# Reordering the last outputs, the softmax and the W products of a fused attention and feed-forward kernel

## The chip, the cores and the metric

The kernel runs on one core of one Trainium2 chip. In it TensorE multiplies matrices and writes the products into PSUM, an on-chip memory; VectorE and ScalarE copy them out of it (an "eviction"); SyncE, ScalarE and GpSimd issue the transfers (DMA) to and from the chip's main memory. The metric is device time in microseconds (us) from start to end; lower is better. Each version is run several times and the median is quoted. One further execution is taken with the hardware profiler; its span is some 1.8 us shorter than the device time of the same execution (569.5 against 571.25 us for the kernel before).

## The reference, cut to what matters

```python
B, N, C = 4, 5824, 256                    # four batches; d_ff is 1024
qn = q / (norm(q, axis=1) + 1e-6);  kn = k / (norm(k, axis=1) + 1e-6)
a  = softmax(kn.transpose(0, 2, 1) @ qn / tau)     # 256 x 256 per batch
x  = (v @ a).reshape(B * N, C)
out = ((x @ w1) * (x @ w2)) @ w3 @ w_out           # 23296 x 256, float32
```

The kernel folds the softmax into w1 and w2 ("fold", giving Wf for each batch), and w3 @ w_out into one matrix W (the "W products"). What is left per row is a = v Wf1, b = v Wf2, and o = (a*b) W. In profile lines, s and e are the scaled scores and their exponential, w is a W product and w3T the transposed w3 that it needs; osb and oleft are the copies of o and of the left rows (below) that are stored.

## The kernel before

TensorE's instructions are written out in one order by a bookkeeping clock. A list of due times (`at`) says at which clock value a piece of softmax, of the scores or of W is put between the a/b steps. Each batch is cut into twelve chunks: eleven of 512 rows, and a small last one of 192 rows, of which 64 are "left rows" that two neighbouring batches share in one output tile.

```python
LAG = 2          # outputs o run this many steps behind a and b
LAG_END = 5      # ... in the last chunk of the last batch

# soft_units(n): (cost, due time after the scores, piece)
return (
    [(0.0, 0.0, norms), (0.0, 6.0, k_row)]
    + [(0.0, 6.0 + 1.3 * i, lambda i=i: k_step(i)) for i in range(4)]
    + [(0.0, 6.5, q_sums), (0.0, 9.3, lambda: q_norm(st["ss"]))]
    + [(0.0, 11.3 + 1.3 * ct, lambda ct=ct: scale(ct)) for ct in range(CT)]
    + [(0.0, 12.0 + 1.3 * ct, lambda ct=ct: exps(ct)) for ct in range(CT)]
    + [(0.2, 16.5, sums)]
    + [(0.43, 17.5 + 1.1 * i, lambda i=i: fold(i)) for i in range(8)]
)
# ... cut ...
def emit_ab(b, c, j):             # 4 matmuls; ScalarE casts a, VectorE multiplies it by b
    # ... cut ...
    nc.scalar.copy(a_sb[:, :n], tiles[0][:, :n])
    nc.vector.tensor_mul(ab, a_sb, tiles[1])
# ... cut ... emit_out, last step of a small chunk:
    nc.scalar.copy(o[:, 0, :], tl[0][:, 0, :])
    other = nc.scalar if b == B - 1 else nc.sync
    other.dma_start(out=rows[:, NT - 1, :], in_=o[:, 0, :])
    if b % 2 == 1:
        nc.vector.tensor_copy(o2, tl[1][:, 0, :])           # the left rows of two batches
        for k, eng in enumerate((nc.sync, other)):
            m = b - 1 + k
            eng.dma_start(out=out[m * N + NT * P : (m + 1) * N, :], in_=o2[k * LEFT : (k + 1) * LEFT, :])
# ... cut ... the main loop
    lag = LAG_END if b == B - 1 and c == NCH - 1 else LAG
    while w_ready[0] and len(pend) > lag and npop < 2:
        emit_out(*pend.pop(0))
# ... and after it
while pend:
    emit_out(*pend.pop(0))
```

Of the kernel before, what the change touches and what calls it, by code (L numbers as in the profile page):

```python
# [15 lines left out]
P = 128  # L16
PIECE = 8
LAG = 2
LAG_END = 5
# [6 lines left out]
def kernel(  # L26
# [12 lines left out]
    nc = tc.nc  # L39
# [204 lines left out]
    def soft_units(n):  # L244
# [37 lines left out]
        def k_step(i):  # L282
            kr = st["kr"]
            nc.scalar.activation(  # L284
                out=kr, in_=kr if i else st["row"], func=(AF.Ln, AF.Exp)[i % 2],
                scale=(1.0, 0.5, 1.0, -1.0)[i], bias=eps_t if i == 2 else 0.0,
            )
# [17 lines left out]
        def q_norm(src):  # L305
            r = work.tile([P, CT], F32, tag="r", name=f"r_{n}", bufs=2)
            nc.scalar.activation(out=r, in_=src, func=AF.Ln)
            nc.scalar.activation(out=r, in_=r, func=AF.Exp, scale=0.5)
            nc.vector.tensor_scalar_add(r, r, 1e-6)
            nc.vector.reciprocal(r, r)  # L310
            if inv_tau != 1.0:
                nc.vector.tensor_scalar_mul(r, r, inv_tau)
            st["r"] = r

        def scale(ct):
            if ct == 0:
                st["s"] = work.tile([P, CT, C], F32, tag="s", name=f"s_{n}", bufs=1)
            nc.vector.tensor_mul(st["s"][:, ct, :], G_tiles[n][:, ct, :], st["kr"])  # L318

        def exps(ct):  # L320
            if ct == 0:
                st["e"] = work.tile([P, CT, C], BF16, tag="e", name=f"e_{n}", bufs=2)
            nc.scalar.activation(  # L323
                out=st["e"][:, ct, :], in_=st["s"][:, ct, :], func=AF.Exp, scale=st["r"][:, ct : ct + 1]
            )
# [49 lines left out]
        def fold(i, tag="ab"):  # L375
            h, rest = divmod(i, 4)
            w, c1 = divmod(rest, 2)
            for c2 in range(CT):
                fold_mm((w, c1, h * 512, (h + 1) * 512), c2, tag, i % 2 == 0 or (n == 0 and i == 7))
# [36 lines left out]
        if n == 0:  # L416
            return [k_first, k_row, q_first, scaled_first, first_folds, second_quarter, sum_start] + [lambda i=i: fold(i) for i in range(4, 8)]

        return (
            [(0.0, 0.0, norms), (0.0, 6.0, k_row)]  # L420
            + [(0.0, 6.0 + 1.3 * i, lambda i=i: k_step(i)) for i in range(4)]
            + [(0.0, 6.5, q_sums), (0.0, 9.3, lambda: q_norm(st["ss"]))]
            + [(0.0, 11.3 + 1.3 * ct, lambda ct=ct: scale(ct)) for ct in range(CT)]
            + [(0.0, 12.0 + 1.3 * ct, lambda ct=ct: exps(ct)) for ct in range(CT)]
            + [(0.2, 16.5, sums)]
            + [(0.43, 17.5 + 1.1 * i, lambda i=i: fold(i)) for i in range(8)]
        )


# [12 lines left out]
    def at(t, cost, fn):  # L442
        seq[0] += 1
        agenda.append((t, seq[0], cost, fn))
# [55 lines left out]
        last_ab[0] = ab  # L500
        clock[0] += 4 * (n * MM_COL + MM_FIX)

    def emit_out(b, c, j, ab):
        small = c == NCH - 1
        if small:
            lhs = [ab[:, :P]]
            if b % 2 == 1:
                lhs.append(lefts[b // 2][:, j, :, :].rearrange("p b t -> p (b t)")[:, P : P + 2 * LEFT])
        else:
            lhs = [ab[:, i * P : (i + 1) * P] for i in range(4)]  # L510
        if j == 0:
            out_tiles[b, c] = [
                psum.tile([P, 2, D], F32, tag="out", name=f"o_{b}_{c}_{h}", bufs=3)
                for h in range(len(lhs) if small else 2)
            ]
        tl = out_tiles[b, c]
        for s, lhsT in reversed(list(enumerate(lhs))) if small else enumerate(lhs):
            h, o = (s, 0) if small else divmod(s, 2)
            nc.tensor.matmul(  # L519
                tl[h][:, o, :], lhsT=lhsT, rhs=W_sb[:, j, :],  # L520
                start=(j == 0 and o == 0), stop=(j == FT - 1 and (small or o == 1)),
                skip_group_check=True,
            )
        clock[0] += len(lhs) * (D * MM_COL + MM_FIX)
        if j == FT - 1:
            o = work.tile([P, 4, D], F32, tag="o_sb", name=f"osb_{b}_{c}", bufs=3)
            rows = out[b * N : b * N + NT * P, :].rearrange("(p i) c -> p i c", i=NT)
            if small:
                nc.scalar.copy(o[:, 0, :], tl[0][:, 0, :])
                other = nc.scalar if b == B - 1 else nc.sync  # L530
                other.dma_start(out=rows[:, NT - 1, :], in_=o[:, 0, :])
                if b % 2 == 1:
                    o2 = work.tile([P, D], F32, tag="kr", name=f"oleft_{b}", bufs=1)
                    nc.vector.tensor_copy(o2, tl[1][:, 0, :])
                    for k, eng in enumerate((nc.sync, other)):
                        m = b - 1 + k
                        eng.dma_start(out=out[m * N + NT * P : (m + 1) * N, :], in_=o2[k * LEFT : (k + 1) * LEFT, :])
            else:
                nc.scalar.copy(o[:, 0:2, :], tl[0])  # L539
                nc.vector.tensor_copy(o[:, 2:4, :], tl[1])  # L540
                nc.sync.dma_start(out=rows[:, 4 * c : 4 * c + 4, :], in_=o)
            del out_tiles[b, c]

    NDEF = 4

# [114 lines left out]
    def make_agenda(b):  # L660
        agenda.clear()
        clock[0] = 0.0
        n = b + 1
        if b == 0:
            at(0.5, 0.87, soft0[5])
            for i in range(4):
                at((1.7, 2.6, 3.5, 3.9)[i], 0.43, soft0[7 + i])
            at(0.0, 0.0, load_library)
            at(4.6, 0.5, lambda: transpose_half_on_pe(0, 0, 1, False))
            at(7.0, 0.5, lambda: transpose_half_on_pe(0, 1, 0, True))  # L670
            at(8.0, 0.5, lambda: transpose_half_on_pe(0, 1, 1, False))
            at(15.0, 0.0, transpose_w3)
            at(15.0, 0.0, lambda: transpose_piece(0, 2))
            for jt in range(FT):
                at(26.0 + 1.2 * jt, 0.87, lambda jt=jt: w_unit(jt))
            moves = [("qk", 1, 0, 29.0), ("v", 0, 3, 30.0), ("v", 0, 4, 30.5), ("qk", 1, 1, 44.0), ("qk", 1, 2, 45.0)]
            moves += [("qk", 1, 3, 53.0), ("qk", 1, 4, 55.0), ("v", 0, 5, 61.0), ("qk", 1, 5, 73.0)]
            moves += [("v", 1, 0, 88.0), ("v", 1, 1, 98.0), ("v", 1, 2, 120.0), ("qk", 2, 0, 130.0)]
            t0, t1 = 54.0, 113.0
        else:  # L680
            moves = [("v", b, 3, 1.0), ("qk", n, 1, 10.0), ("qk", n, 2, 17.0), ("v", b, 4, 26.0), ("qk", n, 3, 38.0)]
            moves += [("v", b, 5, 46.0), ("qk", n, 4, 58.0), ("qk", n, 5, 66.0)]
            moves += [("v", n, 0, 76.0), ("v", n, 1, 86.0), ("v", n, 2, 96.0), ("qk", n + 1, 0, 108.0)]
            moves = [m for m in moves if m[1] < B]
            t0, t1 = 16.0, 98.0

        before = (0, 2) if b == 0 else None
        for nm, m, pi, t in moves:
            if before is not None and not (nm == "v" and before == (m, pi - 1) == (0, 3)):
                at(t, 0.0, lambda w=before: hold(vTs[w[0]][1][:1, 0, :1] if w[1] == NP_ - 1 else vTs[w[0]][0][:1, w[1] * PIECE, 0, :1]))  # L690
            at(t, 0.0, gate)
            if nm == "qk":
                at(t, 0.0, lambda m=m, pi=pi: load_qk(m, pi))
                before = None
            else:
                at(t, 0.0, lambda m=m, pi=pi: load_piece("v", m, pi))
                at(t + 4.0, 0.0, lambda m=m, pi=pi: transpose_piece(m, pi))
                before = (m, pi)
        if n == B:
            agenda.sort()  # L700
            return
        units = score_units(n)
        for i, (cst, fn) in enumerate(units):
            at(t0 + (t1 - t0) * i / len(units), cst, fn)
        soft = soft_units(n)
        for cst, t, fn in soft:
            at(t1 + 1.0 + t, cst, fn)
        agenda.sort()

    for b in range(B):  # L710
        make_agenda(b)
        for c in range(NCH):
            for j in range(FT):
                run_due()
                emit_ab(b, c, j)
                npop = 0
                lag = LAG_END if b == B - 1 and c == NCH - 1 else LAG
                while w_ready[0] and len(pend) > lag and npop < 2:
                    emit_out(*pend.pop(0))
                    npop += 1  # L720
                    run_due()
        run_due(1e9)
    while pend:
        emit_out(*pend.pop(0))


# [33 lines left out]
```

## Time and profile before

| | kernel before |
|---|---|
| device time, median of the first three runs | 571.08 us (570.57 to 572.03) |
| profiled span | 569.5 us |
| TensorE busy | 558.9 us, 98% |
| VectorE, ScalarE busy | 66%, 60% |
| start of the first a | 37.26 us |
| first a to start of the last matmul | 528.10 us |
| start of the last matmul to the start of the trace's last instruction ("tail") | 4.05 us |
| late starts after the first a | 3.08 us in 19 places |

How to read the last row. In the trace every matmul has a start in nanoseconds. A matmul of 512, 256 or 192 columns is followed by the next one after 0.216, 0.109 or 0.082 us when nothing holds it; a later start is counted here as a late start if it is over 0.03 us. In the timeline, bursts of matmuls are merged into one line (x2, x12), and the weight load (PEld) of a late one often bears a bracket with its idle time. The last instruction of the trace is a semaphore event of 0.05 us, so the span ends 0.05 us after the tail.

### The profile page before, as it was taken

Reading aid. Unit: us, or ns where it says so; the run is one execution under the profiler, and the core shown is the slowest. Engines: PE = TensorE matmul, PEld = TensorE weight load, DVE = VectorE, ACT = ScalarE, POOL = GpSimd, SP = SyncE. Lnnn points to the kernel's source line nnn. Section 1 sums busy time; section 2 is a strip of 40 time slices with the busy share of each in tenths; the row PEclk is TensorE's granted clock in tenths of the full one; section 3 lists DMA queues with packets and bytes.
Section 4 is the critical chain, followed back from the end, with each engine's and each line's share of the span. In section 5 each row is a group of like instructions: output and inputs, shape, how many; then the busy total and the mean of one; then the engine's idle time right before and its main releaser. Section 6 shows DMA issues by size and latency. Waiting matters only on the chain.

```text
span 569.5 us, 10098 instructions
## 1 busy us (share of the span) xinstructions
PE 558.9 (98%) x3755; PEld 354.9 (62%) x3755; DVE 375.7 (66%) x581; ACT 340.5 (60%) x627; POOL 77.2 (14%) x163
## 2 busy tenths in 40 slices
PE   8799999999999999999999999999999999999997
PEld 5664576776666666666666666666665656656665
DVE  1047645788966577887766567787866665565564
ACT  1057535777766577777675567777756554454453
POOL 4260013020220110121210111030120000000000
PEclk9999999999999999999999999999999999999999
DMA  9999989978455696595761495766740325221011
GB/s 213 211 175 208 168 170 233 225 171 195 112 147 120 132 194 147 98 184 128 148 148 73 95 217 121 155 120 121 184 112 39 85 74 148 63 70 68 38 73 58
DMA packets 75105, 77.45 MB, mean 136 GB/s; under 512 B 54193, under 2 KB 58801, under 8 KB 75057
## 3 DMA queue, kind: packets, MB, share of 16 engines
q0 software_dynamic: 15760, 38.93, 39.1%
q1 hardware_dynamic: 59072, 37.69, 22.3%
q8 instruction: 29, 0.48, 0.3%
q10 hardware_dynamic: 224, 0.20, 0.1%
q14 instruction: 20, 0.16, 0.1%
HBM read 78.91 MB, written 23.86 MB: 180 GB/s over the span
## 4 chain that ended last, share of the span: by engine, by line
PE 91%; DMA 6%; ACT 1%; DVE 1%; POOL 0%; issue 0%; ACTq 0%; POOLq 0%
PE o L519 28%; PE b L477 27%; PE a L477 27%; PE G L193 5%; DMA k<-in_k_dram 5%; PE fold L364 2%; DMA w3T<-w_wout 1%; PE w L643 1%; ACT kr L284 0%; ACT as L483 0%; PE quarter L390 0%; POOL k L112 0%; DVE s L318 0%; ACT e L323 0%; DVE abs L498 0%
## 5 line engine op out<-in xcount | busy, mean ns | idle before, releaser
L498 DVE TENSOR_TENSOR abs<-as,b 128x512 bf16<-128x512 bf16 x336 | 230.2, 686 | 138.0 <-ACT as L483 124.9
L483 ACT CAST as<-a 128x512 bf16<-128x512 f32 (+1 forms) x384 | 216.2, 563 | 173.4 <-DVE abs L498 87.1
L477 PEld LDWEIGHTS <-Wf 128*128 128x128 bf16 x1536 | 148.8, 98 | 101.7 <-issue 1.8
L477 PE MATMUL a<-vT,Wf 128*128 128x512 bf16 x704 | 209.4, 379 | 0.4 <-ACT Wf L399 0.4
L477 PE MATMUL b<-vT,Wf 128*128 128x512 bf16 x704 | 209.4, 379 | 0.0
L519 PE MATMUL o<-W_sb,abs 128*128 128x256 bf16 x1344 | 201.1, 273 | 0.0
L519 PEld LDWEIGHTS <-abs 128*128 128x128 bf16 x1344 | 131.4, 98 | 80.8
L202 DVE TENSOR_TENSOR acc<-acc,sq 128x1024 f32<-128x1024 f32 x66 | 80.4, 1219 | 0.7 <-ACT sq L190 0.7
L193 PE MATMUL G<-k,q 128*128 128x256 bf16 x276 | 49.6, 273 | 0.0
L190 ACT ACTIVATE sq<-q 128x512 f32<-128x512 bf16 x66 | 41.8, 634 | 0.0
L190 ACT ACTIVATE sq<-k 128x512 f32<-128x512 bf16 x66 | 41.6, 630 | 0.0
L465 POOL COPY gate_t<-abs 1x1 bf16<-1x1 bf16 x39 | 9.4, 241 | 170.1 <-DVE abs L498 168.8
L540 DVE COPY osb<-o 128x512 f32<-128x512 f32 x44 | 30.1, 684 | 0.9 <-PE o L519 0.9
L193 PEld LDWEIGHTS <-q 128*128 128x128 bf16 x276 | 27.0, 98 | 3.1
L539 ACT COPY osb<-o 128x512 f32<-128x512 f32 x44 | 25.8, 586 | 3.8 <-PE o L519 1.8
L469 POOL COPY gate_t<-vT 1x1 bf16<-1x1 bf16 x16 | 3.3, 208 | 162.5 <-DMA vT<-v 162.5
L112 POOL DMA_DIRECT2D q<-in_q_dram x28 | 15.1, 539 | 12.5 <-DMA k<-in_k_dram 5.5
L284 ACT ACTIVATE kr<-row 128x256 f32<-128x256 f32 x1 | 0.4, 384 | 26.0 <-PE row L272 26.0
L371 ACT ACTIVATE Wf<-fold,rs 128x512 bf16<-128x512 f32 x15 | 10.3, 688 | 9.0 <-PE fold L364 9.0
L488 DVE TENSOR_TENSOR left<-as,b 128x192 bf16<-128x192 bf16 x32 | 11.2, 353 | 5.7 <-ACT as L483 3.5
L364 PE MATMUL fold<-w,e 128*128 128x512 bf16 x56 | 14.7, 379 | 0.0
L498 DVE TENSOR_TENSOR abq<-as,b 128x512 bf16<-128x512 bf16 x16 | 10.8, 686 | 5.1 <-ACT as L483 4.6
(98 smaller groups left out, 241.8 us busy)
## 6 DMA issues: line engine op xcount, KB each, us to landing
out_dram<-osb SPq DMA_DIRECT2D x44, 512.0 KB, 3.6
k<-in_k_dram POOLq DMA_DIRECT2D x19, 512.0 KB, 8.6
v<-in_v_dram POOLq DMA_DIRECT2D x19, 512.0 KB, 5.2
q<-in_q_dram POOLq DMA_DIRECT2D x18, 512.0 KB, 6.6
w_wout<-in_moe_w_dram POOLq DMA_DIRECT2D x1, 2048.0 KB, 23.1
k<-in_k_dram POOLq DMA_DIRECT2D x4, 320.0 KB, 7.6
v<-in_v_dram POOLq DMA_DIRECT2D x4, 320.0 KB, 5.3
q<-in_q_dram POOLq DMA_DIRECT2D x3, 320.0 KB, 4.3
```

The lines of the kernel that those rows point to most:

```text
L112: nc.gpsimd.dma_start(out=pieces[nm, n, pi][:, lo:hi, :], in_=qk_main[nm, n][0][:, pi * PIECE + lo : pi * PIECE + hi, :])
L190: nc.scalar.activation(out=dst[:, :, part, :], in_=src[:, o : o + 2, :], func=AF.Square)
L193: nc.tensor.matmul(G[:, ct, :], lhsT=qt[:, i, ct * P : (ct + 1) * P], rhs=kt[:, i, :], start=(pr == 0 and part == 0 and ct == 0), stop=(pr ...
L202: nc.vector.tensor_add(accs[n], accs[n], sqs[0])
L364: nc.tensor.matmul(m, lhsT=st["e"][:, c2, c1 * P : (c1 + 1) * P], rhs=w12[:, c2, w, lo:hi], start=(c2 == 0), stop=(c2 == CT - 1),)
L477: nc.tensor.matmul(t[:, :n], lhsT=Wf[b][:, ct, w, j * P : (j + 1) * P], rhs=rhs_of(b, c, ct), start=(ct == 0), stop=(ct == CT - 1),)
L483: nc.scalar.copy(a_sb[:, :n], tiles[0][:, :n])
L488: nc.vector.tensor_mul(both, a_sb[:, :n], tiles[1][:, :n])
L498: nc.vector.tensor_mul(ab, a_sb, tiles[1])
L519: nc.tensor.matmul(tl[h][:, o, :], lhsT=lhsT, rhs=W_sb[:, j, :], start=(j == 0 and o == 0), stop=(j == FT - 1 and (small or o == 1)), skip ...
L539: nc.scalar.copy(o[:, 0:2, :], tl[0])
L540: nc.vector.tensor_copy(o[:, 2:4, :], tl[1])
```

## The change

Its intent: take out these late starts. (1) W comes later, so that it does not wait for the transposed w3. (2) The due times of softmax and folds lie closer together, so that the folds end before the small chunk. (3) The outputs fall behind gradually in the last whole chunk, so that the small chunk has outputs to fill its steps. (4) The left rows are finished and stored ahead of the last tile, both on SyncE.

```diff
--- before.py
+++ after.py
@@ -417,13 +417,13 @@
             return [k_first, k_row, q_first, scaled_first, first_folds, second_quarter, sum_start] + [lambda i=i: fold(i) for i in range(4, 8)]
 
         return (
-            [(0.0, 0.0, norms), (0.0, 6.0, k_row)]
-            + [(0.0, 6.0 + 1.3 * i, lambda i=i: k_step(i)) for i in range(4)]
-            + [(0.0, 6.5, q_sums), (0.0, 9.3, lambda: q_norm(st["ss"]))]
-            + [(0.0, 11.3 + 1.3 * ct, lambda ct=ct: scale(ct)) for ct in range(CT)]
-            + [(0.0, 12.0 + 1.3 * ct, lambda ct=ct: exps(ct)) for ct in range(CT)]
-            + [(0.2, 16.5, sums)]
-            + [(0.43, 17.5 + 1.1 * i, lambda i=i: fold(i)) for i in range(8)]
+            [(0.0, 0.0, norms), (0.0, 5.5, k_row)]
+            + [(0.0, 5.5 + 1.2 * i, lambda i=i: k_step(i)) for i in range(4)]
+            + [(0.0, 6.0, q_sums), (0.0, 8.5, lambda: q_norm(st["ss"]))]
+            + [(0.0, 10.3 + 1.2 * ct, lambda ct=ct: scale(ct)) for ct in range(CT)]
+            + [(0.0, 11.0 + 1.2 * ct, lambda ct=ct: exps(ct)) for ct in range(CT)]
+            + [(0.2, 14.6, sums)]
+            + [(0.43, 15.6 + 1.1 * i, lambda i=i: fold(i)) for i in range(8)]
         )
 
 
@@ -500,7 +500,8 @@
         last_ab[0] = ab
         clock[0] += 4 * (n * MM_COL + MM_FIX)
 
-    def emit_out(b, c, j, ab):
+    def emit_out(b, c, j, ab, only=None):
+
         small = c == NCH - 1
         if small:
             lhs = [ab[:, :P]]
@@ -515,6 +516,8 @@
             ]
         tl = out_tiles[b, c]
         for s, lhsT in reversed(list(enumerate(lhs))) if small else enumerate(lhs):
+            if only is not None and s != only:
+                continue
             h, o = (s, 0) if small else divmod(s, 2)
             nc.tensor.matmul(
                 tl[h][:, o, :], lhsT=lhsT, rhs=W_sb[:, j, :],
@@ -526,20 +529,22 @@
             o = work.tile([P, 4, D], F32, tag="o_sb", name=f"osb_{b}_{c}", bufs=3)
             rows = out[b * N : b * N + NT * P, :].rearrange("(p i) c -> p i c", i=NT)
             if small:
-                nc.scalar.copy(o[:, 0, :], tl[0][:, 0, :])
-                other = nc.scalar if b == B - 1 else nc.sync
-                other.dma_start(out=rows[:, NT - 1, :], in_=o[:, 0, :])
-                if b % 2 == 1:
+                if b % 2 == 1 and only != 0:
                     o2 = work.tile([P, D], F32, tag="kr", name=f"oleft_{b}", bufs=1)
                     nc.vector.tensor_copy(o2, tl[1][:, 0, :])
-                    for k, eng in enumerate((nc.sync, other)):
-                        m = b - 1 + k
-                        eng.dma_start(out=out[m * N + NT * P : (m + 1) * N, :], in_=o2[k * LEFT : (k + 1) * LEFT, :])
+                    for m in (b - 1, b):
+                        k = (m - b + 1) * LEFT
+                        nc.sync.dma_start(out=out[m * N + NT * P : (m + 1) * N, :], in_=o2[k : k + LEFT, :])
+                if only != 1:
+                    nc.scalar.copy(o[:, 0, :], tl[0][:, 0, :])
+                    other = nc.scalar if b == B - 1 else nc.sync
+                    other.dma_start(out=rows[:, NT - 1, :], in_=o[:, 0, :])
             else:
                 nc.scalar.copy(o[:, 0:2, :], tl[0])
                 nc.vector.tensor_copy(o[:, 2:4, :], tl[1])
                 nc.sync.dma_start(out=rows[:, 4 * c : 4 * c + 4, :], in_=o)
-            del out_tiles[b, c]
+            if only is None:
+                del out_tiles[b, c]
 
     NDEF = 4
 
@@ -672,7 +677,7 @@
             at(15.0, 0.0, transpose_w3)
             at(15.0, 0.0, lambda: transpose_piece(0, 2))
             for jt in range(FT):
-                at(26.0 + 1.2 * jt, 0.87, lambda jt=jt: w_unit(jt))
+                at(27.5 + 1.2 * jt, 0.87, lambda jt=jt: w_unit(jt))
             moves = [("qk", 1, 0, 29.0), ("v", 0, 3, 30.0), ("v", 0, 4, 30.5), ("qk", 1, 1, 44.0), ("qk", 1, 2, 45.0)]
             moves += [("qk", 1, 3, 53.0), ("qk", 1, 4, 55.0), ("v", 0, 5, 61.0), ("qk", 1, 5, 73.0)]
             moves += [("v", 1, 0, 88.0), ("v", 1, 1, 98.0), ("v", 1, 2, 120.0), ("qk", 2, 0, 130.0)]
@@ -714,14 +719,18 @@
                 run_due()
                 emit_ab(b, c, j)
                 npop = 0
-                lag = LAG_END if b == B - 1 and c == NCH - 1 else LAG
+                lag = LAG
+                if b == B - 1 and c >= NCH - 2:
+                    lag = LAG_END if c == NCH - 1 else LAG + (LAG_END - LAG) * (j + 1) // FT
                 while w_ready[0] and len(pend) > lag and npop < 2:
                     emit_out(*pend.pop(0))
                     npop += 1
                     run_due()
         run_due(1e9)
-    while pend:
-        emit_out(*pend.pop(0))
+
+    n = len(pend)
+    for i, only in [(i, 1) for i in range(n - 1)] + [(i, 0) for i in range(n - 2)] + [(n - 1, 1), (n - 2, 0), (n - 1, 0)]:
+        emit_out(*pend[i], only=only)
 
 
 # ---- launch: one core; inputs and outputs as the reference has them ----
```

## The prediction

> **What bounds the kernel now.** I read the page's busy shares first, then the chain of waits that ended last, then the weight loads' waits, and then the timeline at the four places that the diff touches. Busy shares and chain:
>
> ```profile
> PE 558.9 (98%) x3755; PEld 354.9 (62%) x3755; DVE 375.7 (66%) x581; ACT 340.5 (60%) x627; POOL 77.2 (14%) x163
> ...
> PE 91%; DMA 6%; ACT 1%; DVE 1%; POOL 0%; issue 0%; ACTq 0%; POOLq 0%
> ```
>
> TensorE is busy 98% of 569.5 us and carries 91% of the chain; the 6% of DMA is the loading before 30 us, which the change leaves alone. No other engine passes 66%. The change removes no matmul, so it can only win what TensorE loses between matmuls, plus what lies after the last one. A wide matmul (512 columns) starts every 0.216 us when nothing holds it (a pair every 0.43 us in the timeline), a 256-column one every 0.109 us, a 192-column one every 0.082 us. A start later than that is a gap, and the gaps are what I add up. After 45 us they lie in few places.
>
> The W products (timeline of TensorE):
>
> ```profile
> 63.56 0.59 PE L477 MATMUL b<-vT,Wf 128*128 128x512 bf16 x2
> 64.28 1.05 PE L643 MATMUL w<-w_wout,w3T 128*128 128x256 bf16 x8
> ...
> 67.33 0.59 PE L477 MATMUL b<-vT,Wf 128*128 128x512 bf16 x2
> ...
> 68.21 1.92 PE L643 MATMUL w<-w_wout,w3T 128*128 128x256 bf16 x16 [0.29 <-DMA w3T<-w_wout]
> ```
>
> Two wide matmuls from 63.56 end their turn at 63.99, but w starts at 64.28: 0.29 us lost. From 67.33 the turn ends at 67.76 and w starts at 68.21: 0.45 us. The bracket names the transposing DMA of w3T. Sum 0.74 us.
>
> The end of batch 0, in its small last chunk (timeline, all engines):
>
> ```profile
> 178.75 0.74 DVE L373 TENSOR_SCALAR Wf<-fold,rs 128x512 bf16<-128x512 f32 x1
> ...
> 179.12 0.18 PEld L477 LDWEIGHTS <-Wf 128*128 128x128 bf16 x2 [0.18 <-issue]
> ...
> 179.54 0.10 PEld L477 LDWEIGHTS <-Wf 128*128 128x128 bf16 x1 [0.25 <-issue]
> ...
> 179.80 0.10 PEld L519 LDWEIGHTS <-left 128*128 128x128 bf16 x1 [0.16 <-DVE left L488]
> ```
>
> The last eviction of a fold (0.74 us of VectorE) stands in front of the small chunk's products, whose PSUM tiles then come free late. Starts there are late by 0.13, 0.17, 0.26, 0.10 and 0.08 us: 0.74 us.
>
> The softmax of batch 3, during batch 2 (timeline, all engines):
>
> ```profile
> 425.22 0.42 DVE L318 TENSOR_TENSOR s<-G,kr 128x256 f32<-128x256 f32 x1
> 425.67 0.51 ACT L323 ACTIVATE e<-s,r 128x256 bf16<-128x256 f32 x1 [1.09 <-DVE s L318]
> ...
> 427.29 0.42 DVE L318 TENSOR_TENSOR s<-G,kr 128x256 f32<-128x256 f32 x1
> 427.75 0.51 ACT L323 ACTIVATE e<-s,r 128x256 bf16<-128x256 f32 x1 [1.09 <-DVE s L318]
> ...
> 428.78 0.31 PEld L477 LDWEIGHTS <-Wf 128*128 128x128 bf16 x2 [0.22 <-issue]
> ```
>
> Here scale and exp of the same half were emitted into the same step, so ScalarE stands 1.09 us, twice, with the next cast of a behind it; TensorE then finds no free PSUM tile: 0.21 + 0.06 = 0.26 us with the odd nanoseconds. Batch 2's small chunk, at 444 to 446 and with no folds near, has late starts of 0.13 + 0.08 = 0.21 us.
>
> The end of the program (timeline, all engines):
>
> ```profile
> 560.29 0.72 PEld L477 LDWEIGHTS <-Wf 128*128 128x128 bf16 x8 [0.18 <-issue]
> ...
> 561.19 0.10 PEld L477 LDWEIGHTS <-Wf 128*128 128x128 bf16 x1 [0.18 <-issue]
> ...
> 563.17 0.37 PEld L477 LDWEIGHTS <-Wf 128*128 128x128 bf16 x4 [0.19 <-issue]
> ...
> 565.56 0.42 DVE L534 COPY oleft<-o 128x256 f32<-128x256 f32 x1 [0.66 <-PE o L519]
> ...
> 566.01 0.49 SPq L537 DMA_DIRECT2D out_dram<-oleft  x1
> 566.07 0.41 ACTq L531 DMA_DIRECT2D out_dram<-osb  x1
> 566.52 0.53 ACTq L537 DMA_DIRECT2D out_dram<-oleft  x1
> ```
>
> Late starts: 0.19, 0.05, 0.19 us, then 0.18 us at 563.2. The last matmul starts at 565.41, and the span ends 4.05 us later.
>
> **What the Trainium skill says.** "TensorE: Matmul & The Clock Gate", section "Back-to-back issue gap", gives N/2.4 + 2.5 ns when warm: 216, 109 and 82.5 ns for 512, 256 and 192 columns. The trace agrees, with 0.216, 0.109 and 0.082 us. (The same section calls 131 ns the sustained spacing at N=512; this trace contradicts that, and I use the trace.) "PSUM — Partial Sum Buffer", section "Engine vs sequencer instructions", says the queues of ScalarE and VectorE are strict FIFO; the 1.09 us in which ScalarE holds a cast behind an exp agree. "DMA: Bandwidth & Descriptors", section "Issuing engines are not separate DMA queues", says that starting transfers from several engines only saves the time that a sequencer takes to start them. The trace has that time as 0.41 to 0.53 us, and issue to landing as 1.8 us for the last osb and 2.0 us for each left store.
>
> **The change part by part.** I worked the emission order through with the program's own bookkeeping clock (its costs and its list of due times), for both versions. It fixes order only; times are from the trace.
>
> (1) W later by 1.5 on that clock. w0 now follows two more a/b steps (0.863 us each, so 1.73 us). Without the first gap w0 would have come at 63.99; it now comes at about 65.7. Its w3T landed by 64.28, so no wait. Then one a/b step, w1, and w2 at about 68.4, where the second w3T has landed by 68.21: free by 0.1 to 0.2 us. The third and fourth pieces landed by 70.0 and 72.0, and are needed at about 71.0 and 73.6. Gain 0.74 us, of which I take 0.7 for the thin margin. 32 instead of 30 products wait for W; the buffers (16 in the held tiles, 34 others) suffice.
>
> (2) Softmax closer together. In batch 0 the folds now end before its small chunk. What remains there is what batch 2's small chunk shows without folds, 0.21 us, so the gain is 0.74 - 0.21 = 0.53 us; I take 0.5. In batch 2, each exp now falls one a/b step after its scale, so the 0.26 us go. In batch 1 that order was already so and no softmax gap stood there: 0. Against it: in batch 0 scale, exp and the other scale now share a step. One such step alone, at 425.67, did not stop TensorE (the gap came after the second), so I charge 0.05 us.
>
> (3) The end. The lag grows within the last whole chunk, at its third, sixth and eighth step, so three outputs move behind. A step of that chunk without an output takes TensorE 0.863 us, against 0.59 us of ScalarE and 0.69 us of VectorE: no gap. In the small chunk each a/b step (0.33 us) now has an output behind it from the start (0.437 us for four), against 0.32 and 0.35 us of evictions. The first three gaps, 0.43 us, go. The gap at 563.2 stays: the first small output still asks for its PSUM tiles 0.33 us after the last whole one, whose copy takes 0.59 us.
>
> (4) Left rows ahead. Their last matmul is now third from last instead of second, 0.11 us earlier against the end. But both left stores are now issued by SyncE, one behind the other: copy from 0.11 us earlier, so first issue at what would be 565.95, second 0.49 us + about 0.1 us between issues later at 566.55, landing 2.0 us on at 568.55. Before, ScalarE's second issue at 566.57 landed at 568.58. Gain 0 to 0.05 us; I take 0.
>
> Sum: 0.7 + 0.5 + 0.26 - 0.05 + 0.43 + 0 = 1.84 us of 571.08, that is 0.3%: 569.2 us.
>
> **Rivals.** First: the W wait only moves. The transposes are issued one after another from 59.9 to 69.9, and w2's margin is 0.1 us. For it: that margin, and DMA times scatter. Against it: the transposes wait for nothing in the W part. It would leave some 0.3 us, so 569.5. Second: packing the softmax and folds tighter makes ScalarE and VectorE hold PSUM tiles longer, with new gaps in three batches. For it: in a step with two folds VectorE has 0.69 + 0.75 us of the step's 2.16 us, and sum and first fold now share a step, so the first eviction waits for the reciprocal. Against: these pairs of folds cost TensorE nothing at 430 to 439. It would give back up to 0.8 us, so 570.0. Third: left rows on one queue lengthen the tail by another start of a transfer: +0.5 us, 569.7. Against: my sum of the two issue times above. Fourth, the optimist: the tail shrinks by 0.4 us and batch 0's small chunk loses no time at all: 568.6.
>
> **Range and chances.** The rivals span 568.6 to 570.0; the three runs of before spread by 1.5 us (570.57 to 572.03), which puts about 0.5 us on a median. I take 568.2 to 570.4. 2% would be 11.4 us; all gaps after 45 us together are under 3.5 us, so faster by 2% is nearly excluded, and nothing added could cost 11 us: faster 0.01, same 0.985, slower 0.005.
>
> **What would show it.** Right if the trace of after has no late start before w and no bracket of w3T; no gap at the small chunk of batch 0 above 0.13 us; no exp with 1.09 us of wait in batch 2; no late starts in the last chunk but one of 0.18 us; and still about 4.0 us from the last matmul to the end. Wrong if w2 waits again, if new "issue" gaps stand beside the folds, or if the tail differs from 4.05 us by over 0.2 us. TensorE's busy time should stay at 558 to 559 us while the span shrinks.

## The result, and the profile after

Over six runs each, the kernel before has a median of 571.32 us (570.57 to 572.03) and the changed one 570.08 us (569.49 to 571.09). The ratio is 0.998, with an interval of 0.9966 to 0.9994. Ratios are computed as the mean time of one kernel's runs over that of the other's of the same rounds, so they are not quite the ratio of the medians. By the 2% measure the two are the same; the gain is 0.2%, small but clear of noise.

The changed kernel's page, busy shares and chain:

```profile
PE 557.8 (98%) x3755; PEld 354.9 (62%) x3755; DVE 375.5 (66%) x581; ACT 338.6 (60%) x627; POOL 78.3 (14%) x163
...
PE 93%; DMA 5%; ACT 1%; POOL 0%; issue 0%; DVE 0%; ACTq 0%; POOLq 0%
```

The work is the same (3755 matmuls), and TensorE still carries the chain. The span is 568.0 us. From the first a to the last matmul it now takes 526.20 us instead of 528.10: 1.90 us less. But the tail grew from 4.05 to 4.24 us, and the first a started 0.24 us later, long before anything that changed.

The W products in the changed kernel (timeline of TensorE):

```profile
65.47 0.59 PE L477 MATMUL b<-vT,Wf 128*128 128x512 bf16 x2
65.90 1.04 PE L648 MATMUL w<-w_wout,w3T 128*128 128x256 bf16 x8
```

The pair from 65.47 ends its turn at 65.90, and there w starts: no late start. The next three w also start on time.

The softmax put into batch 2 (first fence) and into batch 0 (second fence), from the changed kernel's timeline:

```profile
422.95 0.42 DVE L318 TENSOR_TENSOR s<-G,kr 128x256 f32<-128x256 f32 x1
...
423.51 0.51 ACT L323 ACTIVATE e<-s,r 128x256 bf16<-128x256 f32 x1
```

```profile
164.19 0.51 ACT L323 ACTIVATE e<-s,r 128x256 bf16<-128x256 f32 x1 [1.09 <-DVE s L318]
...
165.71 0.10 PEld L522 LDWEIGHTS <-abs 128*128 128x128 bf16 x1 [0.15 <-issue]
```

In batch 2 the exp (e) no longer waits for its scale (s). In batch 0 it now does, since scale and exp were put into the same step, and an output matmul starts 0.14 us late a little after it. The small chunk of batch 0 (timeline of TensorE):

```profile
178.39 0.33 PE L477 MATMUL a<-vTt,Wf 128*128 128x192 bf16 x2
178.69 0.33 PE L477 MATMUL b<-vTt,Wf 128*128 128x192 bf16 x2
...
179.84 0.33 PE L477 MATMUL a<-vTt,Wf 128*128 128x192 bf16 x2
180.08 0.33 PE L477 MATMUL b<-vTt,Wf 128*128 128x192 bf16 x2
```

A pair of 192-column matmuls takes 0.165 us when nothing holds it, so these two b are late by 0.13 and 0.08 us: 0.21 us of late starts, instead of 0.74.

The end (timeline of the changed kernel, all engines):

```profile
561.51 0.37 PEld L477 LDWEIGHTS <-Wf 128*128 128x128 bf16 x4 [0.19 <-issue]
...
564.24 1.13 SPq L537 DMA_DIRECT2D out_dram<-oleft  x2
564.41 0.38 ACTq L541 DMA_DIRECT2D out_dram<-osb  x1
```

One of the four late starts of the last chunk is left, as expected. The stores tell where the tail grew. First the issues after 565.4 us in the kernel before, then those after 563 us in the changed one; the last number is the median time from issue to landing:

```profile
out_dram<-osb ACTq DMA_DIRECT2D x1, 128.0 KB, 1.8
out_dram<-oleft SPq DMA_DIRECT2D x1, 64.0 KB, 2.0
out_dram<-oleft ACTq DMA_DIRECT2D x1, 64.0 KB, 2.0
```

```profile
out_dram<-oleft SPq DMA_DIRECT2D x2, 64.0 KB, 2.3
out_dram<-osb ACTq DMA_DIRECT2D x1, 128.0 KB, 2.5
```

The same bytes took 0.3 to 0.7 us longer to land.

### The profile page after: what moved, and what is told of

The parts are those of the page before. It is cut to its first block, busy times and chain, and to the rows that moved or that the text cites. A ratio compares the mean times of both kernels' runs of the same rounds, so it can differ in the third digit from the quotient of the medians.

```text
span 568.0 us, 10095 instructions
## 1 busy us (share of the span) xinstructions
PE 557.8 (98%) x3755; PEld 354.9 (62%) x3755; DVE 375.5 (66%) x581; ACT 338.6 (60%) x627; POOL 78.3 (14%) x163
## 4 chain that ended last, share of the span: by engine, by line
PE 93%; DMA 5%; ACT 1%; POOL 0%; issue 0%; DVE 0%; ACTq 0%; POOLq 0%
PE o L522 28%; PE b L477 28%; PE a L477 28%; PE G L193 5%; DMA k<-in_k_dram 5%; PE fold L364 2%; PE w L648 1%; ACT kr L284 0%; PE quarter L390 0%; POOL k L112 0%; POOL q L112 0%; PE sqk L226 0%; PE row L272 0%; PE tr_I-615_616 L135 0%; ACT e L323 0%
## 5 line engine op out<-in xcount | busy, mean ns | idle before, releaser
L465 POOL COPY gate_t<-abs 1x1 bf16<-1x1 bf16 x39 | 10.8, 276 | 169.8 <-DVE abs L498 167.3
```

## The experiments

My theory when I began: the gain is the sum of the late starts that each part removes, less a tail that is longer because two left stores stand behind one another on one queue. Rivals: the tail is scatter; or the gaps move. All runs were in the fast state, except two single looks whose state is unknown. They came in three sets of rounds on three chips (w_only to left_only; after2 to best; late_left to osb_first), each with runs of the kernel before beside them, from which the ratios come. "First a to last matmul" and "tail" are taken from each run's own trace. Four of the traces lack 7 of the 3755 matmul records; holes of exactly one wide matmul (0.216 us) in them are not counted as late starts.

| run | first a at | first a to last matmul | tail | late starts before w | span | ratio to before (interval) |
|---|---|---|---|---|---|---|
| kernel before | 37.26 | 528.10 | 4.05 | 0.74 | 569.5 | |
| the change | 37.50 | 526.20 | 4.24 | 0 | 568.0 | 0.998 (0.9966 to 0.9994) |
| w_only | 37.73 | 527.22 | 4.04 | 0 | 569.0 | 1.0002 (0.9989 to 1.0014) |
| soft_only | 37.70 | 526.67 | 4.05 | 0.12 | 568.5 | 0.9987 (0.9975 to 1.0) |
| lag_only | 37.20 | 527.02 | 4.03 | 0.23 | 568.3 | 0.9991 (0.9978 to 1.0003) |
| left_only | 37.78 | 527.85 | 4.24 | 0.62 | 569.9 | 1.0001 (0.9988 to 1.0015) |
| after2 | 37.42 | 526.12 | 4.22 | 0 | 567.8 | 0.9978 (0.9965 to 0.999) |
| old_queue | 37.24 | 526.42 | 4.32 | 0 | 568.0 | 0.9984 (0.9971 to 0.9998) |
| tail_dve | 37.28 | 526.12 | 4.04 | 0 | 567.5 | 0.9974 (0.9961 to 0.9986) |
| best | 37.17 | 525.62 | 4.04 | 0 | 566.9 | 0.9966 (0.9954 to 0.9979) |
| late_left | 37.14 | 526.13 | 4.11 | 0 | 567.4 | one look |
| one_less | 37.50 | 526.14 | 4.13 | 0 | 567.8 | one look |
| osb_first | 37.51 | 525.64 | 3.86 | 0 | 567.1 | 0.9971 (0.9959 to 0.9983) |

### One part alone, four runs

**w_only**, from the kernel before:

```diff
-                at(26.0 + 1.2 * jt, 0.87, lambda jt=jt: w_unit(jt))
+                at(27.5 + 1.2 * jt, 0.87, lambda jt=jt: w_unit(jt))
```

> The kernel before with the W products 1.5 later on the bookkeeping clock, nothing else. Theory (the two late starts before w are the whole of this part): no late start before any w, the W part 0.74 us shorter, the four gaps of the last chunk (0.61 us) and the 0.74 us of batch 0's small chunk as in the kernel before. Rival (the wait only moves to the second w3T): one late start of 0.1 to 0.4 us is left before w. Time: 0.7 us less under the theory, 0.3 under the rival; both are near the scatter of runs, so the gaps in the trace decide.

The late starts before w are gone, and the rest stands as before. Yet the time did not fall: 570.81 us against 570.82 us. The three other single runs, which leave W early, show why. Here are soft_only and then lag_only, from the timeline of TensorE:

```profile
63.87 0.59 PE L477 MATMUL b<-vT,Wf 128*128 128x512 bf16 x2
64.41 1.05 PE L643 MATMUL w<-w_wout,w3T 128*128 128x256 bf16 x8
```

```profile
63.36 0.59 PE L477 MATMUL b<-vT,Wf 128*128 128x512 bf16 x2
64.02 1.05 PE L643 MATMUL w<-w_wout,w3T 128*128 128x256 bf16 x8
```

In soft_only w is late by 64.41 - 63.87 - 0.43 = 0.11 us (0.12 with nanoseconds), in lag_only by 0.23 us, and in both the third w is on time. So the wait that this part removes differs from execution to execution with the same order of instructions: 0.74, 0.12, 0.23 and 0.62 us in four profiles, 0.43 us on average. The profile that I predicted from held the largest of them. The expected 0.7 us of time is not confirmed by the runs; 0.43 us (a ratio of 0.9992) lies within w_only's interval. The rival is out: none of the nine profiles with W late has a late start before w. It is out with more room than the prediction's 0.1 to 0.2 us: in the changed kernel the second w3T landed at 66.39 us, not at 68.16 as in the kernel before, and the third w, which needs it, started at 68.51. In the nine profiles with W late it landed at 66.5 us at the latest; in three of the four with W early at 67.4 to 68.4. These runs don't show why.

**soft_only**: only the hunk of due times of the change.

```diff
-            [(0.0, 0.0, norms), (0.0, 6.0, k_row)]
+            [(0.0, 0.0, norms), (0.0, 5.5, k_row)]
 ... the other due times of the change
```

> The kernel before with only the new due times of softmax and folds. Theory: the late starts of batch 0's small chunk fall from 0.74 to 0.21 us, those of batch 2's softmax from 0.26 to 0, and a new one of 0.14 us comes in batch 0 where scale, exp and scale share a step: 0.65 us less in all. Rival (tighter packing makes new waits beside the folds that eat the gain): under 0.3 us less. W gaps 0.74 us as before.

The gaps came as expected: 0.13 + 0.08 us in batch 0's small chunk, 0.14 us at 166.0, none at batch 2's softmax; 0.65 us less in all. The medians differ by 0.69 us (570.13 against 570.82), the ratio by 0.13%.

**lag_only**: only the gradual lag.

```diff
-                lag = LAG_END if b == B - 1 and c == NCH - 1 else LAG
+                lag = LAG
+                if b == B - 1 and c >= NCH - 2:
+                    lag = LAG_END if c == NCH - 1 else LAG + (LAG_END - LAG) * (j + 1) // FT
```

> The kernel before with only the gradual lag in the last whole chunk; the last outputs in the old order and on the old queues. Theory: the first three late starts of the last small chunk (0.43 us) are gone, the fourth of 0.18 us stays, the last matmul starts 0.43 us earlier after the first of batch 3, and 4.05 us lie between the last matmul's start and the end as before. Rival (the gaps move into the last whole chunk): 0.43 us of new late starts there, no gain.

Three of the four late starts in the last chunk are gone, 0.18 us is left, none came in the last whole chunk, and the tail is 4.03 us. The medians differ by 0.54 us; the interval of the ratio (0.9978 to 1.0003) just includes no change, so it is the trace that shows this part.

**left_only**: the new order of the last ten matmuls and both left stores on SyncE, nothing else (W, softmax and lag of the kernel before).

> The kernel before with only the new order of the last ten matmuls and both left stores on SyncE. Theory (the two stores one behind the other on one queue beside the osb store lengthen the tail): 4.2 to 4.3 us from the last matmul's start to the end, against 4.05 before, so 0.2 us longer. Rival (the 4.25 us seen after the whole change were a scatter of landings): 4.0 to 4.1 us. All other gaps as in the kernel before.

4.24 us, the same as in the whole change: the longer tail belongs to this part and is no scatter. What in it is at fault (the queue or the order) this run leaves open, since it changes both.

### Which half of part 4, and a better tail

**after2**: the change again, unaltered.

> The whole change a second time, word for word. Theory (gap sizes belong to the order of instructions, the start and w3T's landing to the DMA): 526.2 us from the first a to the last matmul as in its first profile, within 0.1, no late start before w, and again 4.2 to 4.3 us after the last matmul's start. Rival (all of it scatters): these move by 0.3 us or more. Against the kernel before 1.0 to 1.3 us less, the sum of the four parts as the single runs have them: 0.43 us on average for W (0.74, 0.12, 0.23 and 0.62 us stood in four profiles with W early), 0.65 softmax, 0.43 lag, less 0.19 for the tail.

526.12 and 4.22 us: both within 0.1 of the first profile. The medians differ by 1.34 us, 570.76 against 569.42. In the thirteen profiles, all with the same work before it, the first a starts anywhere between 37.14 and 37.78 us, so the 0.24 us of later start in the first profile of the change fall into the scatter of the loads.

**old_queue**: the change, with the second left store on ScalarE behind the store of osb, as in the kernel before (diff condensed).

```diff
-                        nc.sync.dma_start(out=out[m * N + NT * P : (m + 1) * N, :], in_=o2[k : k + LEFT, :])
+                        # for b == B - 1 and m == b: kept back, and after osb's store
+                        nc.scalar.dma_start(out=dst, in_=src)
```

> The whole change, but the second left store goes out on ScalarE behind the osb store, as in the kernel before; the new order of the last matmuls stays. Theory (the longer tail comes of two left stores behind one another on SyncE, beside osb's): 4.0 to 4.1 us from the last matmul's start to the end. Rival (it comes of the new order of matmuls): 4.2 to 4.3 us.

My theory fell: the tail is 4.32 us on the old queues, even longer. The issues of old_queue:

```profile
out_dram<-osb ACTq DMA_DIRECT2D x1, 128.0 KB, 2.5
out_dram<-oleft SPq DMA_DIRECT2D x1, 64.0 KB, 2.3
out_dram<-oleft ACTq DMA_DIRECT2D x1, 64.0 KB, 2.3
```

All three land as late as in the changed kernel. The queue is not at fault. What is left is the order of the last matmuls, which makes the left rows ready 0.11 us earlier. The packets in the traces show a switch. In the kernel before, the first left store is issued 0.65 us after the last matmul's start and osb's 0.71 us after it; osb's packets start first (at 1.62 us), left's at 1.96, and the last packet ends at 2.85 us. In the changed kernel left is issued at 0.54 and osb at 0.71 us; left's packets start first (1.69), osb's at 2.03, and the last packet ends at 3.03 us.

**late_left** tests that: the change, with left's last matmul back at second from last, and both stores still on SyncE.

```diff
-    for i, only in [(i, 1) for i in range(n - 1)] + [(i, 0) for i in range(n - 2)] + [(n - 1, 1), (n - 2, 0), (n - 1, 0)]:
+    for i, only in [(i, 1) for i in range(n - 1)] + [(i, 0) for i in range(n - 1)] + [(n - 1, 1), (n - 1, 0)]:
```

> The whole change, with left's last matmul second from last, where the kernel before had it; both left stores stay on SyncE. Six profiles so far show: where the first left store is issued 0.65 us after the last matmul's start, osb's packets start at 1.61 us, ahead of left's, and 4.03 to 4.05 us pass to the end; where it is issued at 0.54 us, left's packets start first, osb's only at 2.03 us, and 4.22 to 4.32 us pass. Theory (the 0.11 us by which left is earlier change the order of the stores, and that lengthens the tail): osb's packets at 1.6 us again and 4.0 to 4.1 us to the end, even with both left stores on SyncE. Rival (two stores on one queue are at fault after all): 4.2 us or more.

```profile
out_dram<-oleft SPq DMA_DIRECT2D x2, 64.0 KB, 2.0
out_dram<-osb ACTq DMA_DIRECT2D x1, 128.0 KB, 1.8
```

osb's packets start at 1.61 us again, the landings are back at 1.8 and 2.0 us, and the tail is 4.11 us, 0.01 above the range that I had given and 0.11 to 0.13 below that of the change. So it is making the left rows ready 0.11 us earlier that lengthens the tail. With it osb's larger store loses its place in front; that this switch is the reason is likely, but no run changes it alone. Its time is a single run (569.23 us) and proves nothing by itself.

**one_less**: the change without the second of the last left stores, wrong (64 rows of the output are never written, and the comparison says so).

```diff
-                    for m in (b - 1, b):
+                    for m in (b - 1, b) if b < B - 1 else (b - 1,):
```

> The whole change without the second of the last two left stores: wrong in 64 rows on purpose. Theory (the packets of the last stores start one after another, some 0.35 us apart, and the last one sets the end): the end comes with osb's packets, 3.7 to 3.9 us after the last matmul's start, against 4.22 to 4.24. Rival (the two stores that stay set the end): 4.1 us or more.

4.13 us: the rival's figure. osb's packets start at 2.03 us and end at 2.84 us, as in the change. So the third store costs only 0.1 us, and osb's own store is slow: it takes 0.81 us from its first to its last packet (0.82 in the change), against 0.54 us in the kernel before, where its packets go first. Coming behind left's packets does not by itself make it slow: in tail_dve (below) osb comes last of all and takes 0.51 us. There its packets start at 2.33 us, when those of the left stores have ended (2.32); in the change they overlap with the first left store's (osb 2.03 to 2.85 us, left 1.69 to 2.43). Why the overlap costs more in this order these runs don't show.

For the flip itself the traces have a pattern: in all thirteen profiles the store whose issuing instruction ended first started its packets first. Before, SyncE's left issue runs from 0.65 to 1.14 us and ScalarE's osb issue from 0.71 to 1.12, so osb is first; in the change they run from 0.54 to 1.03 and from 0.71 to 1.09, so left is first. No run tests this pattern as a cause.

**tail_dve**: the change, with left's last matmul one place earlier still, both copies on VectorE, the left stores at once on SyncE and ScalarE, osb's last (diff condensed).

```diff
-                    nc.scalar.copy(o[:, 0, :], tl[0][:, 0, :])
+                    (nc.vector.tensor_copy if b == B - 1 else nc.scalar.copy)(o[:, 0, :], tl[0][:, 0, :])
-    ... [(i, 0) for i in range(n - 2)] + [(n - 1, 1), (n - 2, 0), (n - 1, 0)]
+    ... [(0, 0), (1, 0), (n - 1, 1)] + [(i, 0) for i in range(2, n)]
-                        nc.sync.dma_start(out=out[m * N + NT * P : (m + 1) * N, :], in_=o2[k : k + LEFT, :])
+                        eng = nc.scalar if b == B - 1 and m == b else nc.sync
+                        eng.dma_start(out=out[m * N + NT * P : (m + 1) * N, :], in_=o2[k : k + LEFT, :])
```

> The whole change, with another tail: left's last matmul one place earlier, both last copies on VectorE, the left stores at once on SyncE and ScalarE, the osb store last on ScalarE. Theory (the end is the last start of a store plus some 1.9 us): last start 0.95 us after the last matmul's instead of 1.09[...]: 3.6 to 3.8 us to the end. Rival (three stores together take 2.3 us to land whatever their order): 4.1 us or more.

4.04 us: better than the change, but not the 3.6 to 3.8 us of the theory. The last store was issued 1.05 us after the last matmul's start instead of 0.95, and took 2.14 us to land instead of some 1.9.

**best**: tail_dve's tail, and three repairs (only the repairs are shown).

```diff
-                at(27.5 + 1.2 * jt, 0.87, lambda jt=jt: w_unit(jt))
+                at(28.4 + 1.2 * jt, 0.87, lambda jt=jt: w_unit(jt))
-            + [(0.0, 11.0 + 1.2 * ct, lambda ct=ct: exps(ct)) for ct in range(CT)]
+            + [(0.0, 11.7 + 1.2 * ct, lambda ct=ct: exps(ct)) for ct in range(CT)]
+                psum.tile([P, 2, D], F32, tag="G", name=f"o_{b}_{c}_{h}", bufs=1)
+                if small and b % 2 == 1 and h == 0
+                else psum.tile([P, 2, D], F32, tag="out", name=f"o_{b}_{c}_{h}", bufs=3)
```

> The tail of the run before, W at 28.4 for more margin, each exp later by 0.7 so that none shares a step with its scale, and the last small output in the PSUM bank that held the scores, which is free then. Theory: no late start before w, none of 0.14 us at the softmax of batch 0, none of 0.18 us at the left rows of batches 1 and 3; 525.7 us from the first a to the last matmul, 3.7 us after it: 566.9 us of span at a first a of 37.5, against 568.0 for the whole change and 569.5 for the kernel before. Rival (the exps, later, hold up the sums or the folds): a new gap of 0.2 us or more near 165, 294 or 427 us.

The gaps of 0.14 us and 0.18 us (twice) are gone, and 525.62 us lie between the first a and the last matmul. The tail of 3.7 us did not come (4.04). The span of 566.9 us agrees with the forecast because the first a came at 37.17 us, not 37.5, which made up for part of the tail; so that agreement is partly luck. Time: 568.74 us (568.63 to 569.27) against 570.76 us, ratio 0.9966.

**osb_first**: best, with osb's last matmul and copy ahead of left's, osb's copy back on ScalarE and its store first there, and the left stores last on SyncE and ScalarE (diff condensed).

```diff
+    for i, only in [(i, 1) for i in range(n - 3)] + [(i, 0) for i in range(n)] + [(i, 1) for i in range(n - 3, n)]:
```

> The best kernel so far, but osb's last matmul goes ahead by three places and is copied by ScalarE and stored first; left is last, copied by VectorE, its stores at once on SyncE and ScalarE. Theory (stores start their packets one after another, so the earliest issued must be the largest one and the last two must not wait behind it): osb's packets at 1.3 us after the last matmul's start, left's at 1.9 and 2.2, and 3.8 to 3.9 us to the end, against 4.04 in the best kernel: span 566.7 at a first a of 37.2. Rival (the end comes 2 us after the last issue and more, whatever goes before): 4.0 us or more.

```profile
out_dram<-osb ACTq DMA_DIRECT2D x1, 128.0 KB, 1.7
out_dram<-oleft SPq DMA_DIRECT2D x1, 64.0 KB, 2.0
out_dram<-oleft ACTq DMA_DIRECT2D x1, 64.0 KB, 2.2
```

osb's packets start at 1.27 us, those of left at about 1.9 and 2.2, and the tail is 3.86 us, the shortest of all, as forecast. But the run changes two things: the larger store goes in front, and the last issue comes 0.81 us after the last matmul's start instead of 1.05 in best. The last store then took 2.18 us to land, against 2.14 in best, so the earlier last issue accounts for the whole of the shorter tail; that the larger store must be in front is not shown. In time this cannot be told from best (568.78 us, ratio 0.9971, against 568.74 us, 0.9966): the 0.18 us are below the scatter. Both beat the kernel before. Best also lies below the change in the same rounds (568.74 against 569.42 us); osb_first had no timed runs of the change beside it.

## Why the prediction was right or wrong, point by point

The time (569.2 us predicted, 570.08 measured, range 568.2 to 570.4) held. The gain was forecast as 1.84 us and came out as 1.24 us; a further 0.24 us of the miss is the kernel before, whose median rose from 571.08 us in three runs to 571.32 in six. The mechanism of steps 1 to 3 held, with step 1 mis-sized; in step 4 the landing time, taken as unchanged, did not hold.

- **Step 1, W, 0.7 us.** The late starts went, as foretold, and the feared second wait never appeared, though not by the margin worked out: the landing that the working took as fixed (68.21 us) came 1.8 us earlier (66.39), unforeseen. But the size was taken from one profile, and the wait scatters: the mean of the four profiles with W early is 0.43 us. Mis-sized by about 0.3 us.
- **Step 2, softmax, 0.5 + 0.26 - 0.05 = 0.71 us.** It measured 0.65 us. The remaining 0.21 us of batch 0's small chunk and the vanished 0.26 us of batch 2 were right; the shared step of scale and exp in batch 0 costs 0.14 us, not 0.05.
- **Step 3, the lag, 0.43 us.** Right: three late starts gone, 0.18 us left, none new.
- **Step 4, left rows, 0 us.** This failed at "landing 2.0 us on at 568.55". The issues came at 0.54 and 1.09 us after the last matmul's start, where the working had 0.54 and 1.14, but the last landing took 2.3 us: 0.19 us of loss. That lies just inside the prediction's own sign of being wrong (a tail that differs by over 0.2 us). The third rival named a longer tail, but its reason (one queue) is refuted by old_queue; late_left shows that it is left's earlier place among the last matmuls, with which the order of the packets changes.
- **The sum again with the measured terms**: 0.43 + 0.65 + 0.43 - 0.19 = 1.32 us, against 1.24 and 1.34 us between the medians in two sets of rounds. The four single ratios multiply to 0.9981, against 0.998 and 0.9978 for the whole. Nothing of the gain is left unexplained beyond the scatter. But each single part is smaller than the half-width of its ratio's interval (0.0013, or 0.7 us), so the parts rest on the traces, W above all, since w_only's time did not fall.
- **The rivals.** A moved W wait and new gaps beside the folds did not show; the second rival's small form is the 0.14 us of batch 0.
- **A slip in the working.** Its last matmul at 565.41 us, and its 566.57 and 568.58 us for ScalarE's second issue and landing, stand 0.05 us too late: the timeline that it shows has this issue at 566.52, and the trace has the matmul at 565.36 and the landing at 568.53. All are shifted alike, so its differences stay, the tail of 4.05 us too if it is counted to the last instruction's start.

What stays open is why osb's packets take 0.82 us instead of 0.54 when the first left store is already under way, and whether the ends of the issuing instructions decide the order of the packets.

## What to carry to other kernels

In a kernel bound by one engine to 98%, list that engine's late starts one by one; their sum bounds what any reordering can win. Take waits on a DMA from several profiles, since a single one may show almost twice the mean (0.74 against 0.43 us here). At the end of a program, it is the last landing that counts: in all thirteen profiles the tail ends 0.85 to 0.94 us after it. Making a small store ready earlier can push a larger one back, so check every landing after such a change, and bring the last issue forward, as osb_first did.

## What the Trainium skill lacked or had wrong

- "TensorE: Matmul & The Clock Gate", section "Back-to-back issue gap", gives 131 ns as the sustained spacing of pairs of weight load and matmul at N=512. Here 1408 such pairs run at 216 ns when nothing holds them, which is what the page's formula for the isolated gap says (and 109 and 82.5 ns at 256 and 192 columns).
- "DMA: Bandwidth & Descriptors", section "Anatomy of one DMA — SWDGE (gpsimd) path", gives a fixed 2.0 us plus the bytes, for transfers issued by GpSimd. Beyond the interleaving that the prediction cites, no page says what small stores cost each other when SyncE and ScalarE issue them within a few tenths of a microsecond, or which starts its packets first: here 64 KB landed in 2.0 to 2.3 us and 128 KB in 1.7 to 2.5 us, depending on their order and times of issue.
